# A planner that may take later TensorE products first, and single PSUM banks in turn

## The chip, the cores and the metric

The kernel runs on one core of a Trainium2 chip. The metric is the device time of one execution in microseconds (us). A change of about 0.2% can be told from none.

## What is computed

Three parts follow one another: retention (attention with a decaying mask instead of a softmax), a feed-forward layer with a softmax gate and a layer norm, and four experts whose outputs are weighted per token. Cut to what matters:

```python
scores = (q @ k.T) / sqrt(64)                 # 4 sequences of 576 tokens, 8 heads of 64
x = (scores * decay_mask) @ v                 # no softmax; -> 2304 tokens x 512
h = x @ w_in                                  # 512 -> 1024
e = exp(h - max(h)); solu = h * e / (sum(e) + 1e-9)
x2 = layernorm(solu) * g_ln @ w_out           # 1024 -> 512
p = domain_probs / (sum(domain_probs) + 1e-9)
for e in range(4):
    out += p[:, e:e+1] * (relu(x2 @ w1[e]) @ w2[e])   # 512 -> 1024 -> 512
```

## The kernel before

The 2304 tokens are 18 groups of 128 and go through in three passes of six groups (two blocks of 384 tokens). A product in near full precision is made of three matmuls with operands split in a high and a low part (mm3). A pass has these stages:

- h and t: for each group h_mm makes two halves of h in a PSUM tile of two banks (next_a, two such tiles, psA); chain1 to chain3b are the softmax gate and the norm on VectorE, ScalarE and GpSimd; t_mm transposes the result into two banks, t_hi and t_lo (or t_los) split it into hT.
- x2: x2_mm(b, m) makes a 128 x 384 piece of the second projection from hT and wB (24 matmuls, one bank); x2_act, x2_dve and x2_new turn the pieces into the sums B11 ... T4 that the experts multiply with (a Strassen-like scheme of seven products).
- experts: pass one (experts, with l1 and l2_mm) keeps tokens on the partitions in its second layer; passes two and three (experts_s) use the seven products for both layers and take transformed weights back from DRAM. A step of l1 has the products 1, 5, 2, 6, 4 (of the step before), 3, 7, each two times three matmuls of 384 columns. Its PSUM banks are x (for products 1, 6, 7, 4), y (5, 3) and z (2). l2_mm makes 24 matmuls of 512 columns into one bank, and l2_out adds the result to acc.

PSUM has eight banks: three single ones (bt, called b in the profile; next_b takes them in turn), sbank, and four that a pool holds, either as two double tiles (psA) or as four single ones (psX). Opening a pool closes the one before; its tiles wait for the last use of the tiles that lay there.

Retention of the first eleven groups lies in the head of the kernel, whose order is written out by hand (ORDER) and issued directly. The last seven groups (OWN) are taken in during the last expert of pass one and the h stage of pass two: att_pre loads the group and scales v and q on GpSimd, att_first makes the state and the scores (att_st, att_qk), att_last the output (att_pv). Their buffers are tmp and dec in turn.

From the end of the head on, nothing is issued directly: the class Recorder notes each operation with its engine, a modelled cost and the operations it depends on. flush then plays the recorded operations through a model of the engines and issues them in the order that comes out. Every PE operation has a due time, its place on a clock of PE work in program order; other operations are due early enough for what follows them, or 12 us (SLACK) after their place. Each engine takes of its ready operations the one due first, with one exception: TensorE keeps the order of the program,

```python
if e == "PE":
    can = [r for r in can if r[2] is pe[at]]
```

A flush is a border: nothing behind it is planned before anything ahead of it on the same engine. Such borders stand before the last expert's second layer in pass one, before xb is laid out in pass two (i == GP - 1), at the start of experts_s and at its end.

Nearly all instructions have line L144 in the profile, the recorder's call, so tiles tell them apart.

Of the kernel before, what the change touches and what calls it, by code (L numbers as in the profile page):

```python
# [26 lines left out]
GP = NG // NPASS  # L27
TB = GP // 2
# [31 lines left out]
l4 t5 r3 l5 s1 s3  # L60
"""

LATENCY = 0.12
ISSUE = 0.06
FIXED = {"PE": 0.0135, "ACT": 0.13, "DVE": 0.16, "POOL": 0.36, "SP": 2.0}
RATE = {"PE": 1 / 2400, "ACT": 0.93e-3, "DVE": 1.03e-3, "POOL": 1.82e-3, "SP": 4 * P / 300e3}
# [26 lines left out]
class Recorder:  # L93

    def __init__(self, nc):
        self.nc = nc
        self.ops = None
        self.seen, self.count = {}, 0
        self.now = 0.0
        self.free = {e: 0.0 for e in FIXED}  # L100
        self.port = self.dma = 0.0
        self.busy = {}
        for name, engine in ENGINE.items():
            setattr(self, name, Issuer(self, name, engine))

    def start(self):
        self.ops = []

    def note(self, op, ap, write):
        name, runs = spans(ap)  # L110
# [15 lines left out]
    def record(self, name, engine, kind, args, kw):  # L126
        aps = dict(kw)
        aps.update(zip(("out", "in0", "in1") if kind == "matmul" else ("out", "in_"), args))
        outs = [aps[k] for k in ("out", "accum_out") if isinstance(aps.get(k), bass.AP)]
        keys = ("in_", "in0", "in1", "scalar", "scalar1", "scalar2", "bias", "scale")  # L130
        ins = [aps[k] for k in keys if isinstance(aps.get(k), bass.AP)]
        size = lambda ap: int(np.prod([d[1] for d in tuple(ap.ap)[1:]]))
        n = size(aps["out"])
        if engine == "SP" and aps["out"].space == bass.MemoryType.DRAM:
            n = size(aps["in_"])
        elif kind == "tensor_reduce":
            n = size(aps["in_"])
        rate = RATE[engine]
        if engine == "PE" and aps["in0"].dtype == F32:
            rate *= 2 if kw.get("is_transpose") else 4  # L140
        call = getattr(getattr(self.nc, name), kind)
        wide = [a for a in ins if a.space != bass.MemoryType.PSUM and size(a) > 1]
        port = engine == "POOL" or (engine == "DVE" and len(wide) > 1)
        op = Op(engine, lambda: call(*args, **kw), FIXED[engine] + rate * n, port)  # L144
        op.banks = {a.name for a in ins + outs if a.space == bass.MemoryType.PSUM}
        for a in ins:
            self.note(op, a, False)
        for a in outs:
            self.note(op, a, True)
        op.before.discard(op)  # L150
        op.index = self.count
        self.count += 1
        self.ops.append(op)

    def flush(self, done=True):
# [2 lines left out]
        begin = clock  # L158
        inside = set(ops)
        for op in ops:  # L160
            op.after, op.due, op.at = [], None, clock
            if op.engine == "PE":
                op.due = clock
                clock += op.cost
# [24 lines left out]
        while len(order) < len(ops):  # L189
            late = now + 1e-9  # L190
            while waiting and waiting[0][0] <= late:
                op = heapq.heappop(waiting)[2]
                queue[op.engine].append((op.due, op.index, op))
            moved = False
            for e in FIXED:
                if free[e] > late or not queue[e] or (e == "SP" and self.dma > late + DEPTH):
                    continue
                can = [r for r in queue[e] if not (r[2].port and self.port > late)]
                can = [r for r in can if all(busy.get(b, 0) <= late for b in r[2].banks)]
                if e == "PE":  # L200
                    can = [r for r in can if r[2] is pe[at]]
                if not can:
                    continue
                best = min(can)
                queue[e].remove(best)
                op = best[2]
                moved = True
                if e == "PE":
                    at += 1
                    idle += now - max(free[e], begin)  # L210
                if e == "SP":
                    free[e] = now + ISSUE
                    self.dma = max(self.dma, now) + op.cost - FIXED[e]
                    op.end = self.dma + FIXED[e]
                else:
                    op.end = free[e] = now + op.cost
                if op.port:
                    self.port = op.end
                for b in op.banks:
                    busy[b] = op.end if e == "PE" else op.end + LATENCY  # L220
                op.start = now
                order.append(op)
                for s in op.after:
                    left[s] -= 1
                    ready_at[s] = max(ready_at[s], op.end + (0 if s.engine == e != "SP" else LATENCY))
                    if not left[s]:
                        heapq.heappush(waiting, (ready_at[s], s.index, s))
            if not moved:
                times = [*free.values(), self.port, self.dma - DEPTH, *busy.values(), *(w[0] for w in waiting[:1])]
                now = min(t for t in times if t > late)  # L230
# [17 lines left out]

SLACK = 12.0
DEPTH = 2.0  # L250
TRACE = []


@with_exitstack
def retention_solu_moe(
# [19 lines left out]
    big = ctx.enter_context(tc.tile_pool(name="big", bufs=1))  # L275
    drp = ctx.enter_context(tc.tile_pool(name="drp", bufs=1, space=bass.MemoryType.DRAM))
    psB = ctx.enter_context(tc.tile_pool(name="psB", bufs=1, space=bass.MemoryType.PSUM))
    stack = ExitStack()
    ctx.enter_context(stack)
    pool = {}  # L280

    def open_pool(name, bufs):
        stack.close()
        new = stack.enter_context(tc.tile_pool(name=name, bufs=1, space=bass.MemoryType.PSUM))
        width = 2048 // bufs
        pool["a"] = [new.tile([P, width], F32, tag=f"a{i}", name=f"{name}_{i}") for i in range(bufs)]
        pool["n"] = 0

    bt = [psB.tile([P, 512], F32, tag=f"b{i}", name=f"b{i}") for i in range(3)]
    sbank = psB.tile([P, 512], F32, tag="s", name="sbank")  # L290
    turn = [0]
    open_pool("psA0", 2)

    def next_a():
# [3 lines left out]
    def next_b():  # L298
        turn[0] += 1
        return bt[turn[0] % 3]  # L300

    def quad(t):
        return t.rearrange("p (n t) -> p n t", n=4)
# [224 lines left out]
            eng.tensor_tensor(out=t[:, 2560:3072], in0=t[:, 2560:3072], in1=t[:, 0:512], op=ALU.mult)  # L528

    def att_qk(g):  # L530
        t = grp(g)
        qt, kt = (t[:, i : i + 512].rearrange("p (n t) -> p n t", n=NP) for i in (0, 512))
        qk = [quad(next_b()) for a in range(2)]
# [13 lines left out]
        att[g] = ret  # L547

    def att_st(g):
        t = grp(g)  # L550
        kn, vd = (t[:, i : i + 512].rearrange("p (h t) -> p h t", h=H) for i in (1024, 2048))
        j = g % NJ
# [13 lines left out]
                copy(states[(g + 1) % 2][r, :, r], st_ps[r])  # L566

    def att_pv(g):
        t = grp(g)
        v = t[:, 1536:2048].rearrange("p (h t) -> p h t", h=H)  # L570
        qd = t[:, 2560:3072].rearrange("p (n t) -> p n t", n=NP)
# [68 lines left out]
    ln = {}  # L640

    def h_mm(g, n):
        if n == 0:
            hps[g] = next_a()
        ps = hps[g][:, 512 * n : 512 * n + 512]
# [53 lines left out]
    tps = {}  # L699

    def t_mm(g):
        y = exs[:, g % 3]
        if g % GP < (TB if g < GP else TB + 1):
            tps[g] = [quad(next_b()) for _ in range(2)]
        else:
            t = next_a()
            tps[g] = [quad(t[:, 512 * u : 512 * u + 512]) for u in range(2)]
# [45 lines left out]
    x2ps = {}  # L753

    def x2_mm(b, m):
        lt = hT[b]
        sl = slice(m * P, m * P + P)
        ps = next_b()[:, 0:BLK]
        for f in range(KF):
            w = wB[:, f]  # L760
            mm3(ps, (w[:, 0, sl], w[:, 1, sl]), (lt[:, 0, f], lt[:, 1, f]), f == 0, f == KF - 1)
# [120 lines left out]
    steps = {}  # L882

    def prod(s, i, bank, more=False):
        a, b = PRODUCTS[i]
        for kk in range(2):
            mm3(
# [17 lines left out]
    def l1(s, i):  # L905

        m = s % NM
        if i == 1:
            x = next_a()[:, 0:BLK]
            y, z = (next_b()[:, 0:BLK] for _ in range(2))  # L910
            steps[s] = (x, y, z)
        x, y, z = steps[s]
        if i == 1:
# [44 lines left out]
    FORDER = [0, 4, 1, 5, 2, 6, 3, 7]  # L958

    def l2_mm(ps, b, t, fs, first, last):  # L960
        sl = slice(t * P, t * P + P)
        for f in fs:
            h, w = hT[b], wB[:, f]
# [5 lines left out]
    def experts(p):  # L969
        for e in range(E):  # L970
# [9 lines left out]
                        l1(s - 1, 4)  # L980
                        w1_next(s + 2)
            last = s0 + NM - 1
            first = next_b()
            l2_mm(first, 1, 0, FORDER[:2], True, False)
            l1(last, 4)
            w1_next(last + 3)
# [10 lines left out]
            for b in (1, 0):  # L997
                for t in range(TB):
# [1 line left out]
                        ps, first = first, None  # L1000
                        l2_mm(ps, b, t, FORDER[2:], False, True)
                    else:
                        ps = next_b()
                        l2_mm(ps, b, t, FORDER, True, True)
                    l2_out(p, e, b * TB + t, ps)
                    if e + 1 == E:
# [59 lines left out]
    def experts_s(p):  # L1066
        wBf = wB.rearrange("p f s t -> p (f s t)")
        hTf = [t.rearrange("p s k t -> p (s k t)") for t in hT]
        nc.flush()
        open_pool(f"psX{p}", 4)  # L1070
        nc.start()
        xs = [t[:, 0:BLK] for t in pool["a"]]
        ys = [t[:, 0:BLK] for t in bt]
        zs = [sbank[:, 0:BLK]]
# [18 lines left out]
        at = {}  # L1093

        def mms(kind, k, i, ks):
            if (k, i) not in at:
                at[k, i] = used[kind]
                used[kind] += 1
# [147 lines left out]
                        x_load(p + 1, g)  # L1246
        nc.flush()
        if p + 1 < NPASS:
            open_pool(f"psA{p}", 2)
            nc.start()  # L1250

    OWN = list(range(EARLY, NG))
# [32 lines left out]
    def second(p, g0):  # L1285

        if p == 0:
            raw = tmp[:, 2048:3072]
            w1_load(0)
            w1_load(1, raw)  # L1290
            xb_region()
            nc.start()
            w1_ops(0)
            w1_ops(1, raw)
        else:
            for m in range(4):
                x2_mm(0, m)
                x2_act(m)
# [16 lines left out]
    with tc.manual_schedule():  # L1315
# [43 lines left out]
            atoms[atom[0]](int(atom[1:]))  # L1359
        second(0, None)  # L1360
        experts(0)
        for p in range(1, NPASS):
            g0 = p * GP
            own = p == 1
# [119 lines left out]
```

## Time and profile before

| | |
|---|---|
| median of 3 runs | 1041.54 us (1040.85 to 1042.57) |
| profiled execution | 1042.08 us |
| its span, first to last instruction | 1040.3 us |
| TensorE matmuls | 6188, busy 1008.3 us (97%) |
| VectorE, ScalarE, GpSimd busy | 617.3, 526.9, 445.6 us |
| mean granted TensorE clock | 0.996 of 2.4 GHz |

The profiled execution is one run; the differences below are taken against it. A matmul's end in the profile is modelled, and neighbours overlap, so the count of matmuls in a stretch tells more than the busy share. PEld is TensorE's weight load, which runs ahead of the matmuls. Idle time in brackets behind an instruction is that of its engine just before it, with the instruction that ended it.

### The profile page before, as it was taken

The page shows a single profiled execution, that of the slowest core. Times are in us where ns is not written, and L with a number is a line of the kernel's source. Part 1 is how long each engine was busy: PE and PEld are TensorE (multiplying, and loading weights), DVE is VectorE, ACT ScalarE, POOL GpSimd, SP SyncE. Part 2 cuts the span into 40 slices and gives each one's busy share as a digit, 9 for nine tenths or more (in the row PEclk, how much of TensorE's full clock was granted, in tenths as well). Part 3 has the DMA queues.
Part 4 walks back from the last instruction along what each step waited for, and adds up shares of the span by engine and source line. Part 5 has one row for each costly group of instructions (what it writes and reads, how often), then busy time and mean ns, then how long its engine had stood idle before and what let it go on. Part 6 is the DMA issues. An engine that isn't in the chain of part 4 may idle for free.

```text
span 1040.3 us, 17080 instructions
## 1 busy us (share of the span) xinstructions
PE 1008.3 (97%) x6188; PEld 947.0 (91%) x6188; DVE 617.3 (59%) x1038; ACT 526.9 (51%) x1032; POOL 445.6 (43%) x433
## 2 busy tenths in 40 slices
PE   4899999999999999999999999999999999999998
PEld 3788998898988987889999999999899999999998
DVE  6999686585774513643735656475444636556564
ACT  4568664262533402563745556473573746555462
POOL 2333354333635011321465655654230465655553
PEclk9999999999999999999999999999999999999999
DMA  9857689999785858551757666577640847566524
GB/s 343 343 186 257 216 293 313 309 292 336 227 270 185 280 226 304 203 200 59 232 152 226 184 195 211 157 270 248 243 152 18 250 134 244 163 216 193 184 72 134
DMA packets 122788, 226.79 MB, mean 218 GB/s; under 512 B 9936, under 2 KB 57040, under 8 KB 116560
## 3 DMA queue, kind: packets, MB, share of 16 engines
q1 hardware_dynamic: 122704, 225.70, 65.2%
q8 instruction: 49, 0.80, 0.3%
q14 instruction: 35, 0.29, 0.1%
HBM read 169.00 MB, written 62.95 MB: 223 GB/s over the span
## 4 chain that ended last, share of the span: by engine, by line
PE 51%; issue 1%; DVE 0%; ACT 0%; POOL 0%; POOLq 0%; ACTq 0%
PE psX L144 26%; PE b L144 16%; PE sbank L144 6%; PE psA L144 3%; DVE acc L144 0%; POOL acc L144 0%; DVE stats L144 0%; ACT psA L144 0%; ACT acc L144 0%; DVE tmp L144 0%; ACT xb L144 0%; ACT xa L144 0%; ACT tmp L144 0%; POOLq L144 0%; ACTq L144 0%
## 5 line engine op out<-in xcount | busy, mean ns | idle before, releaser
L144 POOL TENSOR_TENSOR h<-tmp,h 128x384 fp32r<-128x384 f32 x128 | 128.7, 1015 | 95.9 <-ACT h L144 82.1
L144 PE MATMUL b<-xa,wA 128*128 128x384 f32 x672 | 132.8, 335 | 2.3 <-DVE h L144 1.2
L144 PE MATMUL b<-wB,h 128*128 128x512 f32 x576 | 133.0, 390 | 1.3 <-POOL wB L144 1.3
L144 PEld LDWEIGHTS b<-wB,h 128*128 128x128 f32 x576 | 107.8, 188 | 24.2 <-POOL wB L144 2.2
L144 POOL TENSOR_TENSOR wA<-wA 128x512 fp32r<-128x512 f32 x74 | 97.2, 1321 | 68.0 <-ACT wA L144 65.0
L144 PEld LDWEIGHTS b<-xa,wA 128*128 128x128 f32 x672 | 117.7, 188 | 3.5 <-DVE h L144 2.1
L144 PE MATMUL psX<-xb,wA 128*128 128x384 f32 x576 | 112.6, 336 | 0.1
L144 PEld LDWEIGHTS psX<-xb,wA 128*128 128x128 f32 x576 | 100.4, 188 | 2.7 <-DVE b L144 2.3
L144 POOL TENSOR_TENSOR tmp<-tmp 128x256 f32<-128x256 f32 (+1 forms) x68 | 61.9, 925 | 72.0 <-DMA tmp<-in_w 50.0
L144 ACT ACTIVATE h<-tmp 128x384 fp32r<-128x384 f32 x144 | 72.9, 521 | 33.7 <-DVE tmp L144 33.7
L144 PE MATMUL b<-h,wB 128*128 128x384 f32 x480 | 85.1, 336 | 0.0
L144 PEld LDWEIGHTS b<-h,wB 128*128 128x128 f32 x480 | 83.0, 188 | 0.1
L144 PE MATMUL psX<-h,wA 128*128 128x384 f32 x408 | 74.9, 334 | 0.0
L144 DVE TENSOR_TENSOR sbank<-sbank,tmp 128x384 f32<-128x384 f32 x48 | 27.2, 566 | 77.4 <-PE sbank L144 54.3
L144 ACT ACTIVATE wA<-wA 128x512 fp32r<-128x512 f32 x74 | 46.3, 632 | 51.5 <-DMA wA<-sw 41.7
L144 ACT ACTIVATE tmp<-b 128x384 f32<-128x384 f32 x104 | 51.1, 491 | 41.8 <-DVE b L144 17.1
L144 PEld LDWEIGHTS psX<-h,wA 128*128 128x128 f32 x408 | 71.1, 188 | 0.0
L144 PE MATMUL psA<-wA,xa 128*128 128x512 f32 x288 | 70.2, 399 | 0.8 <-DVE tmp L144 0.7
L144 DVE TENSOR_TENSOR b<-b,tmp 128x384 f32<-128x384 f32 x80 | 45.0, 563 | 41.1 <-PE b L144 38.0
L144 PEld LDWEIGHTS psA<-wA,xa 128*128 128x128 f32 x288 | 53.6, 190 | 13.3 <-DVE tmp L144 1.0
L144 POOL TENSOR_TENSOR wC<-wC 128x512 fp32r<-128x512 f32 x38 | 50.6, 1337 | 31.8 <-ACT wC L144 31.8
L144 DVE SCALAR_TENSOR_TENSOR tmp<-b,tmp 128x384 f32<-128x384 f32 x96 | 51.2, 554 | 16.9 <-ACT tmp L144 8.5
(239 smaller groups left out, 1984.4 us busy)
## 6 DMA issues: line engine op xcount, KB each, us to landing
wA<-sw SPq DMA_DIRECT2D x298, 256.0 KB, 3.0
sw<-wA SPq DMA_DIRECT2D x32, 896.0 KB, 7.7
tmp<-in_w SPq DMA_DIRECT2D x24, 512.0 KB, 5.7
grps<-in_qkv SPq DMA_DIRECT2D x10, 1024.0 KB, 6.5
wC<-sw SPq DMA_DIRECT2D x38, 256.0 KB, 2.8
sw<-wCf SPq DMA_DIRECT2D x32, 256.0 KB, 3.3
wA<-sin SPq DMA_DIRECT2D x8, 1024.0 KB, 6.7
wB<-sout SPq DMA_DIRECT2D x8, 1024.0 KB, 8.0
```

The source lines that it names most:

```text
L144: op = Op(engine, lambda: call(*args, **kw), FIXED[engine] + rate * n, port)
```

## The change

- Costs: LATENCY 0.15 instead of 0.12; a float32 matmul that is no transpose costs 2 instead of 4 units per column; a VectorE operation with two operands in SBUF costs 1.2 times as much.
- Order on TensorE: mark() numbers the products (each att_, h_, t_, x2_, prod and l2 call is a group). The planner may now take any ready PE operation up to 150 recorded operations (AHEAD) behind the first one not issued, and stays in a group it has begun while it has something ready there.
- Pass one's experts: the pool of four banks is opened as four single tiles (psX0) ahead of x2's second block, and x, y, z and the second layer's banks come from next_x, which goes round the seven banks psX and bt. x2's second block uses it too.
- After pass one's experts: a flush, and psA1 is opened as two double tiles.
- Passes two and three: the flush and the opening of the single tiles move from the start of experts_s to the start of second, ahead of x2. There x2's first block and the last two transposed groups use next_s (bt and sbank in turn), its second block next_x.

The diff, cut to its core:

```diff
-LATENCY = 0.12
+LATENCY = 0.15
...
         if engine == "PE" and aps["in0"].dtype == F32:
-            rate *= 2 if kw.get("is_transpose") else 4
+            rate *= 2
...
+        rate *= 1.2 if engine == "DVE" and port else 1.0
...
                 if e == "PE":
-                    can = [r for r in can if r[2] is pe[at]]
+                    while at < len(pe) and pe[at].start is not None:
+                        at += 1
+                    can = [r for r in can if r[2].index <= pe[at].index + AHEAD]
+                    can = [r for r in can if r[2].group == self.last] or can
...
+AHEAD = 150
...
+    def next_s():
+        turn[2] += 1
+        return (bt + [sbank])[turn[2] % 4]
+
+    def next_x():
+        turn[1] += 1
+        return (pool["a"] + bt)[turn[1] % 7]
...
     def t_mm(g):
+        nc.mark()
         y = exs[:, g % 3]
-        if g % GP < (TB if g < GP else TB + 1):
+        if g >= GP and g % GP >= GP - 2:
+            tps[g] = [quad(next_s()) for _ in range(2)]
+        elif g % GP < (TB if g < GP else TB + 1):
             tps[g] = [quad(next_b()) for _ in range(2)]
...
     def x2_mm(b, m):
+        nc.mark()
...
-        ps = next_b()[:, 0:BLK]
+        ps = (next_b if nc.ops is None else next_x if b else next_s)()[:, 0:BLK]
...
         if i == 1:
-            x = next_a()[:, 0:BLK]
-            y, z = (next_b()[:, 0:BLK] for _ in range(2))
+            x, y, z = (next_x()[:, 0:BLK] for _ in range(3))
...
-            first = next_b()
+            first = next_x()
...
-                        ps = next_b()
+                        ps = next_x()
...
     def experts_s(p):
-        nc.flush()
-        open_pool(f"psX{p}", 4)
-        nc.start()
...
         if p + 1 < NPASS:
-            open_pool(f"psA{p}", 2)
+            open_pool("psA2", 2)
...
             xb_region()
+            open_pool("psX0", 4)
             nc.start()
             w1_ops(0)
             w1_ops(1, raw)
         else:
+            nc.flush()
+            open_pool(f"psX{p}", 4)
+            nc.start()
             for m in range(4):
                 x2_mm(0, m)
...
         experts(0)
+        nc.flush()
+        open_pool("psA1", 2)
+        nc.start()
```

## Rows read from the trace of the kernel before

**Rows 1.** Page, part 1: busy us of each engine, share of the span, instructions.

```profile
PE 1008.3 (97%) x6188; PEld 947.0 (91%) x6188; DVE 617.3 (59%) x1038; ACT 526.9 (51%) x1032; POOL 445.6 (43%) x433
```

**Rows 2.** Busy us (instructions) by stretch and engine, clock, DMA share, GB/s.

```profile
125.00:385.00 260.00, 255.84 (x1288) 230.51 (x1288) 161.82 (x266) 103.97 (x200) 102.55 (x97) 1.00 0.85 279
385.00:455.00 70.00, 66.67 (x618) 55.31 (x618) 32.95 (x55) 27.93 (x49) 15.09 (x23) 0.98 0.54 203
497.00:728.00 231.00, 230.85 (x1326) 229.37 (x1324) 131.39 (x240) 127.45 (x264) 130.52 (x114) 1.00 0.66 210
...
800.00:1036.00 236.00, 234.90 (x1349) 233.32 (x1348) 134.17 (x244) 130.26 (x270) 130.83 (x115) 1.00 0.57 176
```

**Rows 3.** Waits of TensorE, 120 to 1040 us: us in total, times, longest.

```profile
PE sbank L144 <- POOL tmp L144: 2.4, 1, 2.4
PE b L144 <- POOL wB L144: 1.3, 2, 0.7
PE b L144 <- DVE h L144: 1.2, 2, 0.7
PE psA L144 <- DVE h L144: 1.1, 1, 1.1
PE b L144 <- ACT xb L144: 1.1, 1, 1.1
PE b L144 <- DVE tmp L144: 0.9, 2, 0.7
PE psA L144 <- DVE tmp L144: 0.7, 1, 0.7
PE psA L144 <- ACT tmp L144: 0.5, 1, 0.5
```

**Rows 4.** Chain that ended last: start us, us, what; two undisturbed pieces.

```profile
498.00 1.04 PE b L144 x6
...
753.07 5.47 PE psA L144 x24
```

**Rows 5.** Timeline 340 to 343 us: start, us, engine, operation [idle before].

```profile
340.19 1.21 PE L144 MATMUL psA<-xb,wA 128*128 128x384 f32 x6
...
342.50 1.34 PE L144 MATMUL psA<-xa,wA 128*128 128x384 f32 x6 [1.10 <-DVE h L144]
```

**Rows 6.** Timeline 214 to 217 us: two starts where the weight load idled shortly.

```profile
214.45 1.01 PEld L144 LDWEIGHTS psA<-xa,wA 128*128 128x128 f32 x6 [0.30 <-DVE h L144]
214.45 1.32 PE L144 MATMUL psA<-xa,wA 128*128 128x384 f32 x6
...
216.71 1.00 PEld L144 LDWEIGHTS b<-xa,wA 128*128 128x128 f32 x6 [0.22 <-DVE h L144]
```

**Rows 7.** Timeline 389 to 407 us, and the stretch 400 to 420 us.

```profile
389.69 1.01 SPq L144 DMA_DIRECT2D wB<-sout  x2
...
394.32 0.37 SPq L144 DMA_DIRECT2D tmp<-in_qkv  x1
...
395.36 1.16 PE L144 MATMUL b<-dec 64*128 64x128 f32 x16
...
402.70 1.04 POOL L144 TENSOR_TENSOR tmp<-tmp,tabs 128x512 f32<-128x512 f32 x1 [23.83 <-DMA tmp<-in_qkv]
...
404.41 1.96 PE L144 MATMUL b<-tmp 64*128 64x128 f32 x16
...
406.30 4.01 PE L144 MATMUL psA<-wA,xa 128*128 128x512 f32 x13
...
400.00:420.00 20.00, 17.58 (x164) 14.74 (x161) 8.33 (x13) 6.17 (x11) 6.57 (x9) 0.91 0.79 305
```

**Rows 8.** Timeline at 496.7 us, start of pass two's experts.

```profile
496.66 1.01 PEld L144 LDWEIGHTS psX<-xb,wA 128*128 128x128 f32 x6 [0.41 <-ACT tmp L144]
```

**Rows 9.** Timeline 458 to 464 us: x2's start in pass two.

```profile
458.01 6.27 PE L144 MATMUL b<-h,wB 128*128 128x384 f32 x34
...
461.51 1.28 DVE L144 TENSOR_TENSOR h<-b,h 128x512 fp32r<-128x512 f32 x2
```

More of the change, by code (lines that the diff above doesn't have):

```diff
@@ L98, in __init__ @@
         self.seen, self.count = {}, 0
+        self.group, self.last = 0, None
         self.now = 0.0
@@ L107, in start, with mark @@
         self.ops = []
+    def mark(self):
+        self.group += 1
     def note(self, op, ap, write):
@@ L150, in record @@
         op.before.discard(op)
+        op.group = self.group
         op.index = self.count
@@ L160, in flush @@
         for op in ops:
-            op.after, op.due, op.at = [], None, clock
+            op.after, op.due, op.at, op.start = [], None, clock, None
             if op.engine == "PE":
@@ L208, in flush @@
                 if e == "PE":
-                    at += 1
+                    self.last = op.group
                     idle += now - max(free[e], begin)
@@ L277, in retention_solu_moe @@
     psB = ctx.enter_context(tc.tile_pool(name="psB", bufs=1, space=bass.MemoryType.PSUM))
+    turn = [0, 0, -1]
     stack = ExitStack()
@@ L287, in open_pool @@
         pool["n"] = 0
+        turn[1] = -1
     bt = [psB.tile([P, 512], F32, tag=f"b{i}", name=f"b{i}") for i in range(3)]
     sbank = psB.tile([P, 512], F32, tag="s", name="sbank")
-    turn = [0]
     open_pool("psA0", 2)
@@ L568, in att_pv @@
     def att_pv(g):
+        nc.mark()
         t = grp(g)
@@ L642, in h_mm @@
     def h_mm(g, n):
+        nc.mark()
         if n == 0:
@@ L701, in t_mm @@
     def t_mm(g):
+        nc.mark()
         y = exs[:, g % 3]
-        if g % GP < (TB if g < GP else TB + 1):
+        if g >= GP and g % GP >= GP - 2:
+            tps[g] = [quad(next_s()) for _ in range(2)]
+        elif g % GP < (TB if g < GP else TB + 1):
             tps[g] = [quad(next_b()) for _ in range(2)]
@@ L755, in x2_mm @@
     def x2_mm(b, m):
+        nc.mark()
         lt = hT[b]
         sl = slice(m * P, m * P + P)
-        ps = next_b()[:, 0:BLK]
+        ps = (next_b if nc.ops is None else next_x if b else next_s)()[:, 0:BLK]
         for f in range(KF):
@@ L884, in prod @@
     def prod(s, i, bank, more=False):
+        nc.mark()
         a, b = PRODUCTS[i]
@@ L960, in l2_mm @@
     def l2_mm(ps, b, t, fs, first, last):
+        nc.mark()
         sl = slice(t * P, t * P + P)
@@ L1095, in mms @@
         def mms(kind, k, i, ks):
+            nc.mark()
             if (k, i) not in at:
```

## The prediction

> **What bounds the kernel now.** I read the busy table first: TensorE is busy for 97% of the span [rows 1], so no other engine's work is worth anything unless TensorE waits for it. Then the table by stage, to see where its idle time lies behind the hand-ordered head (0 to 125 us): pass one's experts keep it busy for 255.84 of 260 us, the attention of the tokens that follow for 66.67 of 70, while the experts of passes two and three have 230.85 of 231 and 234.90 of 236 [rows 2]. The diff leaves the head's order alone (it is issued directly, without the planner), so the head's idle time is no part of the sum. Then TensorE's own waits from 125 us on: those shown add up to 2.4 + 1.3 + 1.2 + 1.1 + 1.1 + 0.9 + 0.7 + 0.5 = 9.2 us, in eleven waits [rows 3]. That is all the change can work on, apart from what a wait costs beyond its idle time.
>
> That extra has to be priced, because a busy TensorE is modelled. A product of six 384-column matmuls advances the chain by 1.04 us (0.173 each) when nothing is in the way [rows 4]. Round a wait, the product before it is booked with 1.21 us, 0.17 of it tail that would have overlapped, and the product after it with 1.34, so 0.13 more [rows 5]. The waiting matmul also holds back the weight load behind it. So a wait costs its idle time plus about 0.17 + 0.11 = 0.28 us (0.11 is what the second start loses, 1.34 - 1.21 rounded down). I use 0.28 for each.
>
> **The change part by part.**
>
> *Single banks in pass one.* Before, a step's products sat in one of two double-width tiles (x) and two of three single banks (y, z); the next step's y or z is a bank just left. Rows 5 show what that does: the matmul into psA at 342.50 waits 1.10 us until VectorE has read the step before out of that tile. Waits of this kind are "b, DVE h" (1.2 us, two) and "psA, DVE h" (1.1 us, one) [rows 3]: 2.3 + 3 x 0.28 = 3.1 us. Two shorter ones show only in the weight load's idle time, 0.30 and 0.22 us [rows 6]; less the tail of 0.17 and plus the 0.11 of the second start (1.32 against 1.21 again) that is 0.24 and 0.16: 0.4 us. With seven banks in turn, the bank for a new product was last used more than two steps (over 14 us) ago, so all 3.6 us should go. Bounds: 2.6 (one wait kept) to 3.6; I take 3.6. The second layer of pass one gets the same seven banks; its evictions already keep up, so nothing.
>
> *Later work first, in pass one.* The waits for data are "b, POOL wB" (1.3 us, two: the split second-layer weights come late) and "psA, ACT tmp" (0.5, one): 1.8 + 3 x 0.28 = 2.6 us [rows 3]. Free banks let TensorE take the next tile's ready products meanwhile. But the instruction order is fixed when the program is written, so a wait is filled only if the planner's costs foresee it. The change makes VectorE's two-operand work dearer and the latency 0.15, which helps; GpSimd's cost is untouched. Bounds 0 to 2.6; I take half, 1.3.
>
> *The stall at 403.8.* This is the dearest one: TensorE idles 2.4 us for GpSimd, which idles until 402.70 for a transfer into tmp that SyncE issued at 394.32, behind two 1 MB loads issued at 389.69 [rows 3, 7]. The granted clock of 400 to 420 us is 0.91 [rows 7]: a stretch at the 1.2 GHz level follows the idle time. Its cost: the qk group takes 1.96 us against 1.16, and thirteen matmuls 4.01 us where 24 take 5.47 with their tail left out (0.228 each, so 2.96 + 0.17 = 3.13): 0.80 + 0.88 = 1.7 us [rows 4, 7]. Together 2.4 + 0.28 + 1.7 = 4.4 us. Two parts act on it. The planner may now put half an h product (12 x 0.228 = 2.7 us) ahead of the waiting state product. And a new flush after pass one puts the four 1 MB loads behind the tmp load in SyncE's order, so that the latter has the DMA engines to itself; what moves behind it is needed only at x2, 50 us later. Bounds 1.7 (only the clock's part) to 4.4; I take 4.0.
>
> *Attention's next wait*, "b, DVE tmp" (0.9 us in two, so 1.2 with one refill of 0.28) [rows 3]: h products are ready, if the planner sees the wait. 0 to 1.2; I take 0.7.
>
> *x2 and the experts in one plan.* Before, a flush stood between them. The waits there are "b, ACT xb" (1.1 + 0.28) [rows 3] in pass three and one in pass two that shows as 0.41 us of idle time of the weight load [rows 8], 0.41 - 0.17 + 0.11 = 0.35 us by the same working. B11 and B21 are ready long before, so other products can go first: 0 to 1.7; I take 1.2.
>
> *What it adds.* First, the new pool after pass one must wait for the last evictions, as pass three's does now ("psA, DVE tmp", 0.7 + 0.28) [rows 3]. Here two attention groups stand between the last expert tile and the first h product, so nothing; without that cover 0 to 1.0. Second, the fresh rotation of x2's banks: counting the turns, the first x2 product of pass two takes b0, where the second half of a transposed group was just written. In the trace that x2 product starts at 458.01, while VectorE reads that half until 461.51 + 1.28 = 462.8 [rows 9]. In program order this would hold TensorE, and everything queued behind it on TensorE, for 4.8 us + 0.28 = 5.1. The planner knows the bank and can take the next x2 product first (24 x 0.173 = 4.2 us): 0.6 to 0.9 is left. Bounds 0 to 5.1; I take 0.6. Third, products moved forward start just when the plan calls them ready, with no slack. The trace doesn't show such starts; the nearest row is the shortest breaks [rows 6, 8], 0.2 to 0.3 us each. Bounds 0 to 20 of them (5.6 us); I take 7, 2.0 us. The moved flushes themselves issue no instruction; ScalarE, VectorE and GpSimd have idle time to take them [rows 2].
>
> Sum: -3.6 - 1.3 - 4.0 - 0.7 - 1.2 = -10.8, and +0.6 + 2.0 = +2.6, net **-8.2 us**. The profiled execution took 1042.08 us (span 1040.3, 1.8 around it), the median run 1041.54. From the profiled one 1033.9, from the median 1033.3; I say 1033.4. The best end is all gains and no cost, -3.6 - 2.6 - 4.4 - 1.2 - 1.7 = -13.5, so 1028.0.
>
> **The rivals.** *Slower: slack lost in the dense stages.* From 497 to 728 and 800 to 1036 us TensorE runs 2675 matmuls in 467 us, 0.1746 each against the undisturbed 0.173 [rows 2, 4]; that is about 340 products with next to nothing to win. If the planner, with its new costs, thinks one late that is not, it moves another forward that is ready only on paper, and TensorE waits on the chip with all later products queued behind it. A wait of 0.3 us costs 0.3 + 0.28 = 0.58; 14 of them (one in 24) eat the 8.2 us, 25 make it 1042.1 - 8.2 + 14.5 = 1048.4. For it: the plan's costs are averages, and VectorE's order is rebuilt too. Against it: where the head of the order is ready and due first it keeps its place, and a program order that runs here without a wait is mostly ready in the plan as well. *It doesn't do what it says.* The planner sees none of the waits, so the order stays and only banks and flushes act: -3.6 - 1.7 + 1.0 + 3.5 (most of the blocked x2 product) = -0.8, so 1041.2. For it: waits of half a microsecond are below what such costs foresee. Against it: the 2.4 us stall is far above that.
>
> *The clock.* Half a microsecond to a microsecond of idle time in pass one left the granted clock at 1.00 [rows 2, 3]; only the stage with the 2.4 us stall fell. The Trainium skill (TensorE: Matmul & The Clock Gate, A second HAM failure mode) tells of a kernel that cycled through PSUM banks and fell back in clock through small idle gaps, which speaks against this change; the dense stages rotate through all eight banks at a clock of 1.00 [rows 2], so the trace doesn't agree. Were more small gaps to bring one stretch at 1.2 GHz into each of the four experts of pass one, each at the 1.7 us above: 1033.4 + 6.8 = 1040.2.
>
> **How the numbers follow.** Forecast 0.68 (alone 1028.0 to 1038.5), no effect 0.12, lost slack 0.16, clock 0.04. The range runs from the best end, 1028.0, to 1042.0: it takes in the forecast, the no-effect case and the clock, and leaves out most of the slack case and a little below. A measurement of this kernel tells 0.2%, 2.1 us, from no change: faster is under 1039.5, slower over 1043.6. Faster: the forecast less a little, and some of the others, 0.70. Same: most of the no-effect and clock cases and the mild part of lost slack, 0.14. Slower: 0.16.
>
> **What would show it.** Right: no wait for "DVE h" in pass one; clock 1.00 from 400 to 420 us; TensorE busy near 259 of 260 us in pass one's experts; the x2 products of pass two's start swapped. Wrong: new waits of b, psX or sbank in the dense stages (lost slack); the same waits as before outside the banks' (no effect); a stall near 458 us of some 5 us; a granted clock below 1.00 in new places.

## The result and the profile after

| | before | changed |
|---|---|---|
| median (runs) | 1041.68 us (6) | 1030.74 us (6) |
| lowest to highest | 1035.68 to 1042.57 | 1028.85 to 1033.13 |
| ratio, 95% interval | | 0.9904 [0.9877, 0.9932] |
| second comparison | 1039.7 us (7) | 1029.41 us (4), 0.9897 [0.9882, 0.9912] |
| profiled execution, its span | 1042.08, 1040.3 | 1028.85, 1027.1 |

The change saves 10.9 us (10.3 in the second comparison); 8.2 were forecast, and 1030.7 lies in the range of 1028.0 to 1042.0. Ratios here and below are of means, so they differ a little from the quotients of the medians. The instructions on TensorE are the same 6188 matmuls. First the busy table and TensorE's waits behind 120 us (in us: total, times, longest) of the changed kernel, to be held against [rows 1, 3]:

```profile
PE 1006.8 (98%) x6188; PEld 949.4 (92%) x6188; DVE 616.2 (60%) x1038; ACT 526.4 (51%) x1032; POOL 448.4 (44%) x433
```

```profile
PE psA L149 <- DVE tmp L149: 0.6, 1, 0.6
PE b L149 <- DVE h L149: 0.5, 1, 0.5
PE psA L149 <- ACT psA L149: 0.2, 1, 0.2
```

Of the eleven waits with 9.2 us, and a twelfth of 0.2 us (psA for ScalarE's psA) that [rows 3] leave out, three with 1.3 us are left. Two of the three stood there before (0.7 and 0.2); the one of 0.5 us for VectorE's h, in pass three, is new. None is in pass one's experts or in attention. The table by stretch (busy us and instructions of PE, PEld, DVE, ACT, POOL; granted clock; DMA share; GB/s) shows the same:

```profile
125.00:375.00 250.00, 250.00 (x1273) 228.46 (x1273) 161.48 (x264) 101.35 (x198) 98.98 (x96) 1.00 0.86 288
375.00:444.00 69.00, 68.89 (x623) 56.02 (x622) 31.69 (x53) 27.52 (x48) 15.41 (x24) 1.00 0.55 203
486.50:716.00 229.50, 229.50 (x1326) 229.46 (x1324) 132.36 (x242) 128.69 (x267) 131.62 (x115) 1.00 0.67 211
790.00:1024.00 234.00, 232.96 (x1344) 232.64 (x1343) 134.96 (x246) 130.26 (x270) 131.36 (x115) 1.00 0.58 178
```

And the first of these stretches of the kernel before:

```profile
125.00:375.00 250.00, 245.84 (x1244) 222.23 (x1244) 160.49 (x265) 103.97 (x200) 99.01 (x94) 1.00 0.87 285
```

Read the counts, not the busy time: in 250 us of pass one TensorE gets 1273 matmuls done instead of 1244. The dense stage of pass two takes 229.5 us for the 1326 matmuls that took 231 [rows 2].

Since ends of matmuls are modelled, I also work out lost time. It is a matmul's start less the undisturbed pitch of all matmuls ahead of it (0.1733 us for 384 columns, 0.2267 for 512, 0.1092 for a transposed block, 0.0555 and 0.0295 for attention's two small shapes). Taken at the same amount of work, it shows by stage where two executions part, whatever the order. It is worked out from the traces and is no view of the profile:

```
lost us within       before  before   changed changed  program order,
                     (1st)   (again)  (1st)   (again)  free bank (e11)
head                 30.6    32.5     29.2    28.8     31.2
pass one's experts    7.6     7.5      0.6     1.5      5.4
attention, h          9.9     8.4      7.9     7.9      6.8
x2 of pass two        0.6     0.5      0.5     0.5      0.2
dense, pass two       1.1     1.1      0.0     0.0      1.5
h, x2 of pass three   3.2     3.2      2.6     2.6      1.9
dense, pass three     5.3     5.4      4.3     4.3      5.6
whole span           58.3    58.7     45.1    45.7     52.7
```

Pass one's experts are taken from the second block of its x2 on, where the planner begins. Attention ends with the last transposed group ahead of the first x2 product, x2 with the first products of the experts behind it; the last dense stage holds the 4.3 us behind the last matmul too. The head is the same code in all of them and differs by up to 4 us; over all executions of this study it loses 28.5 to 33.3. That is why single spans (here 13.2 us apart) say less than the medians, and why a comparison of stages behind the head is sharper than one of times.

### The profile page after: what moved, and what is told of

Same layout as the page of the kernel before. It is cut to its first block, busy times and chain, and to the rows that moved or that the text cites. A ratio compares the mean times of both kernels' runs of the same rounds, so it can differ in the third digit from the quotient of the medians.

```text
span 1027.1 us, 17077 instructions
## 1 busy us (share of the span) xinstructions
PE 1006.8 (98%) x6188; PEld 949.4 (92%) x6188; DVE 616.2 (60%) x1038; ACT 526.4 (51%) x1032; POOL 448.4 (44%) x433
## 4 chain that ended last, share of the span: by engine, by line
PE 93%; DVE 4%; DMA 2%; ACT 1%; SPq 0%; issue 0%; ACTq 0%
PE psX L149 44%; PE b L149 29%; PE sbank L149 8%; PE psA L149 6%; DMA dec<-in_w_in 1%; DMA sx<-wA 1%; PE b L382 1%; PE b L384 1%; PE b L383 1%; PE b L604 1%; DVE wA L387 1%; PE psA L383 1%; PE psA L382 1%; PE b L610 1%; PE psA L384 0%; PE b L557 0%
## 5 line engine op out<-in xcount | busy, mean ns | idle before, releaser
L149 PE MATMUL psX<-xb,wA 128*128 128x384 f32 x738 | 143.7, 334 | 0.0
L149 PEld LDWEIGHTS psX<-xb,wA 128*128 128x128 f32 x738 | 129.4, 188 | 0.3
L149 PE MATMUL b<-xa,wA 128*128 128x384 f32 x564 | 111.0, 334 | 0.0
L149 PEld LDWEIGHTS b<-xa,wA 128*128 128x128 f32 x564 | 99.0, 188 | 0.1
L149 ACT ACTIVATE tmp<-psX 128x384 f32<-128x384 f32 x122 | 59.5, 489 | 53.0 <-PE psX L149 51.1
L149 POOL TENSOR_TENSOR tmp<-tmp 128x256 f32<-128x256 f32 (+1 forms) x68 | 56.9, 853 | 57.1 <-DMA tmp<-in_w 38.3
L149 PE MATMUL psX<-wB,h 128*128 128x512 f32 x336 | 78.9, 390 | 0.0
L149 PE MATMUL psX<-xa,wA 128*128 128x384 f32 x396 | 77.4, 334 | 0.0
L149 ACT ACTIVATE tmp<-b 128x384 f32<-128x384 f32 x108 | 53.1, 492 | 42.5 <-DVE b L149 18.4
L149 PEld LDWEIGHTS psX<-wB,h 128*128 128x128 f32 x336 | 63.0, 188 | 12.8
L149 PEld LDWEIGHTS psX<-xa,wA 128*128 128x128 f32 x396 | 69.5, 188 | 0.2
```

## The experiments

All ratios are to the kernel before, run on the same chip beside the kernel in question.

**Second profiles.** Both kernels unchanged.

> The kernel before, unchanged, for a second profile of it. Theory one (the 2.4 us stall with its slow stretch is a fixed part of the kernel): a wait for GpSimd's tmp of 2 us or more and a granted clock under 0.95 between 400 and 420 us, as in the first profile. Rival (the stall's size and the slow stretch differ from execution to execution, which is why the added flush didn't show in the time): a wait under 1.5 us, or a clock of 1.00 there; all other waits behind 125 us within 0.2 us of the first profile.

> The changed kernel, unchanged, beside the next two on the same chip. Theory one: 9 to 12 us less than the kernel before, TensorE busy for all of pass one, the three waits behind 125 us of its first profile again (0.6, 0.5 and 0.2 us). Rival (the first result was half luck of the head): under 7 us.

The changed kernel came out at 0.9897 [0.9882, 0.9912]; its waits are those of the first profile with one more, in pass one:

```profile
PE psX L149 <- DVE h L149: 0.6, 1, 0.6
```

The product starts at 335.68, when VectorE has read a tile of the pool into h (an operation of 0.55 us from 335.07 on). So even with seven banks in turn a wait of the kind that the banks should cure can stand there; e5 and e6 below have one too, of 0.7 and 0.6 us. The kernel before showed another picture at the stall:

```profile
PE sbank L144 <- POOL tmp L144: 1.4, 1, 1.4
...
PE sbank L144 <- POOL dec L144: 0.8, 1, 0.8
```

```profile
400.00:420.00 20.00, 17.75 (x175) 14.61 (x174) 8.16 (x13) 6.17 (x11) 7.12 (x9) 1.00 0.87 330
```

The wait is 1.4 us instead of 2.4, another of 0.8 has joined it, and the granted clock is 1.00 where the first profile had 0.91 [rows 7]. The other waits agree within 0.2 us. So the stretch at 1.2 GHz, 1.7 us of my sum, belonged to one execution and not to the kernel.

**Program order (e1).**

```diff
-AHEAD = 150
+AHEAD = 0
```

> The changed kernel with AHEAD at 0, so that TensorE keeps the program's order again; banks, costs and flushes stay as changed. Theory one (banks and order each carry a part): pass one's bank waits stay gone (3.6 us), but its waits for data return (up to 2.6), attention's waits return in part (about 2), the first x2 product of pass two is held by its bank for about 5 us, and the step from x2 to the experts waits again (about 1.5): some 11 us above the changed kernel, 1040 to 1043 us, no gain over the kernel before. Rival (banks and costs did it, the order adds little): 1031 to 1033 us.

1042.64 us, 1.0021 [1.0007, 1.0035]: slower than the kernel before, so theory one holds for the time. Not for all its parts: pass one loses 5.1 us and x2 of pass two 6.2, but attention loses 6.7, less than the changed kernel's 7.9, and no wait of 1.5 us stands between x2 and the experts. The timeline of TensorE at x2's start in pass two (start us, us, engine, operation, idle time before) shows the dearest part:

```profile
453.18 1.03 PE L149 MATMUL b<-tabs,acc 128*128 128x128 f32 x8
458.81 9.91 PE L149 MATMUL b<-h,wB 128*128 128x384 f32 x48 [4.59 <-DVE h L149]
```

The first x2 product waits until VectorE has read the transposed group out of its bank. The granted clock of 444 to 486 us is 0.96 in this run, so part of it ran at 1.2 GHz, as behind the stall in the first profile.

**Program order, free bank (e11).** As e1, and x2's rotation starts one bank further on in pass two:

```diff
             nc.flush()
             open_pool(f"psX{p}", 4)
+            turn[2] = 1 - p
             nc.start()
...
-AHEAD = 150
+AHEAD = 0
```

> TensorE in the program's order (AHEAD at 0) with x2's bank rotation of passes two and three starting at a bank that is free; else as changed. Theory one (what the program's order lost against the kernel before at x2's start was the blocked bank alone, 4.6 us of idle time and 0.3 of restart): that wait goes, 4.9 us less than the run in program order, so a ratio to the kernel before of 0.9965 to 0.9985, which is what banks, costs and flushes are worth without the free order. Rival (the wait moves to the next x2 product, which queues behind the same evictions): a new wait for VectorE's h of over 2 us within 10 us of x2's start, and a ratio above 1.0.

1034.27 us, 0.9951 [0.9930, 0.9973]. The wait went and no other came in its place, so theory one holds in kind. In size the step from e1 to e11 is 0.0070, 7.3 us, more than the 4.9 expected: the trace puts 6.0 us of it at x2's start (6.2 us lost there in e1, 0.2 here), of which 4.6 + 0.3 are the wait. The rest fits the clock, which is 1.00 again; in e1 the 48 matmuls behind the wait take 9.91 us, 1.4 more than undisturbed (48 x 0.1733 and 0.17 of tail).

```profile
444.00:486.00 42.00, 42.00 (x267) 40.37 (x266) 18.11 (x32) 22.06 (x41) 10.60 (x13) 1.00 0.43 155
```

Banks, costs and flushes alone are therefore worth some 5 us once the rotation does no harm, and the free order another 5 (0.9951 against 0.9904 and 0.9897). By the table that is 4.4 us in pass one and 2.8 in the dense stages; attention goes the other way and loses 1.1 more with the free order, and x2 loses 1.0 more in the two passes, where e11 also has the free bank. In pass one the free order cures what banks can't. These waits for data are left there in e11,

```profile
PE b L149 <- POOL wB L149: 1.4, 2, 1.0
...
PE b L149 <- DVE xb L149: 0.9, 1, 0.9
...
PE psX L149 <- POOL wB L149: 0.7, 1, 0.7
```

while no wait for VectorE's h is left there. From the first product of the experts on, pass one loses 3.7 us in e11 against 6.9 and 6.8 before: 3.1 us for the banks, together with the new costs, which no run takes apart here. Ahead of that product e11 loses 1.0 more than before (the wait for xb is new), so over the whole stage 2.1 us are left.

**Old banks in pass one (e2).** Free order, costs and flushes as changed:

```diff
-        ps = (next_b if nc.ops is None else next_x if b else next_s)()[:, 0:BLK]
+        ps = (next_b if len(pool["a"]) == 2 else next_x if b else next_s)()[:, 0:BLK]
...
-            x, y, z = (next_x()[:, 0:BLK] for _ in range(3))
+            x = next_a()[:, 0:BLK]
+            y, z = (next_b()[:, 0:BLK] for _ in range(2))
...
-            first = next_x()
+            first = next_b()
...
-                        ps = next_x()
+                        ps = next_b()
...
-            open_pool("psX0", 4)
```

> The changed kernel, but pass one keeps its banks of before: two double tiles for x, three single banks for y, z and the second layer. Order, costs and flushes as changed. Theory one: the bank waits of pass one return, at most their 3.6 us, less what TensorE can fill with other work: 1032.5 to 1034.5 us, and waits for VectorE's h in the profile between 125 and 375 us. Rival (with a free order the banks no longer matter): 1030.5 to 1031.5 us and TensorE busy for all of pass one.

1029.50 us, 0.9909 [0.9880, 0.9938]: the time of the changed kernel, so the rival is right on the time. In the trace one wait is left in pass one,

```profile
PE b L149 <- ACT wB L149: 1.1, 1, 1.1
```

and the stretch from 125 to 375 us has 1265 matmuls, between the 1244 of before and the 1273 of the changed kernel. No wait for VectorE's h is among them. With a free order TensorE finds other work while a bank is read; the seven banks are then worth 1 to 2 us at most (2.4 us lost in pass one against 0.6 to 1.5). In the time even that is hidden, since attention loses 6.6 us in e2 and not 7.9.

**Old costs (e3).**

```diff
-LATENCY = 0.15
+LATENCY = 0.12
...
-            rate *= 2
+            rate *= 2 if kw.get("is_transpose") else 4
...
-        rate *= 1.2 if engine == "DVE" and port else 1.0
```

> The changed kernel with the planner's old costs (latency 0.12, float32 matmuls at 4 units, VectorE's two-operand work without the 1.2). Theory one (foresight by the costs fills the waits for data): one to three of those waits return, 1 to 2.5 us: 1031.5 to 1033 us. Rival A (costs don't matter): 1030 to 1031.5 us. Rival B (the costs are the main part, since without them the free order puts work where it isn't ready): over 1036 us.

1033.02 us, 0.9936 [0.9915, 0.9957], 3.3 us above the changed kernel's first ratio, with intervals that overlap (that of the second comparison lies just below). The trace has three kinds of waits that the changed kernel doesn't have, so theory one, at the upper end of its range:

```profile
PE b L148 <- ACT tmp L148: 1.4, 1, 1.4
PE sbank L148 <- POOL tmp L148: 0.9, 1, 0.9
...
PE b L148 <- DVE tmp L148: 0.6, 3, 0.3
```

These with 0.28 each are 4.3 us of waits, of which the stages behind the head show about 1.3 as more lost time than the changed kernel's; how much of the 3.3 is the costs stays open between 1.3 and 3.3.

**Less reach (e7).**

```diff
-AHEAD = 150
+AHEAD = 40
```

> The changed kernel with AHEAD at 40 recorded operations instead of 150. At the start of the second pass's x2 the next product that could stand in for the blocked one lies about 64 operations behind it. Theory one (what is gained in pass one needs only the next product or two, and x2's swap needs the long reach): pass one stays within 1 us of the changed kernel's, the wait for VectorE's h at x2's start in pass two is back at 3.5 to 5 us, 1033 to 1036 us if the kernel before takes 1040. Rival (40 reaches everything): within 1.5 us of the changed kernel, 1029 to 1031.5.

1039.92 us, 1.0000 [0.9988, 1.0012]: the whole gain is gone, more than theory one expected. Pass one keeps most of its part (248.18 of 250 us busy, 1268 matmuls), but loses 2.6 us, 1.1 to 2.0 more than the changed kernel where at most 1 was expected; attention loses 1.2 more. The wait at x2's start is back with the expected length, but x2 loses 8.2 us against 0.5, because of the clock and a second wait of 0.5 us:

```profile
457.80 15.24 PE L149 MATMUL b<-h,wB 128*128 128x384 f32 x72 [4.60 <-DVE h L149]
```

```profile
444.00:486.50 42.50, 37.36 (x215) 35.43 (x214) 12.84 (x22) 18.24 (x33) 9.56 (x12) 0.92 0.41 146
```

A mean of 0.92 with two levels means that 16% of these 42.5 us, 6.8 us, ran at 1.2 GHz. Part of that falls into the wait itself: the 72 matmuls behind it take 15.24 us where 72 x 0.1733 and 0.17 of tail make 12.65, so 2.6 us were lost on top of the wait. TensorE gets 215 matmuls done there, the changed kernel 250.

**The flush alone (e4).** The kernel before with one line more:

```diff
         experts(0)
+        nc.flush()
+        nc.start()
         for p in range(1, NPASS):
```

> The kernel before with one flush added after pass one's experts; nothing else. Theory one (SyncE's order cures the 2.4 us stall at 403.8 and the slow stretch behind it, since the four 1 MB loads now come behind the load into tmp): 3 to 4.4 us less than before, 1037.3 to 1038.7 us, and a clock of 1.00 in that stretch. Rival (only TensorE's free order cures it): 1041 to 1042 us, the wait for GpSimd's tmp still over 1.5 us.

1040.30 us, 1.0007 [0.9994, 1.0021]. In its trace the wait for GpSimd's tmp is 0.8 us and the clock did not fall, as theory one has it, but the time doesn't move. The second profile of before explains most of this: against its 1.4 and 0.8 us there is little to cure. Lost time shows that little: attention loses 7.3 us in e4, against 9.9 and 8.4 before, and 1.2 us is less than these times can tell. The step "SyncE's order cures a stall of 4.4 us" was built on an unlucky execution.

**Attention as one group (e5).**

```diff
     def att_qk(g):
-        nc.mark()
         t = grp(g)
...
     def att_st(g):
-        nc.mark()
         t = grp(g)
```

> The changed kernel with the state, score and output products of neighbouring attention groups in one group for the planner, so that TensorE goes from the 512-column products to attention's small shapes 7 times instead of 13 in the second pass's h stage. Theory one (each such excursion costs about 0.3 us in starts, which is where most of the attention part of the gain went): 1.5 to 2 us less than the changed kernel. Rival (the products are put together where the transfers and GpSimd haven't come yet): new waits for GpSimd's tmp or dec of over 0.5 us, and a time equal or longer.

1031.82 us, 0.9921 [0.9897, 0.9945], not shorter. Theory one falls, and not by the rival's waits either: none for tmp or dec is there. The excursions did become fewer, 8 instead of 12, but the 432 small matmuls take 28.4 us in them instead of 26.0. Timelines of one excursion of 64 in the kernel before (again), and in this one:

```profile
394.77 1.09 PE L144 MATMUL b<-tmp 128*64 128x128 f32 x16
395.69 1.04 PE L144 MATMUL b<-tmp,st 128*64 128x128 f32 x16
396.57 0.63 PE L144 MATMUL sbank<-dec 128*64 128x64 f32 x16
397.13 1.16 PE L144 MATMUL b<-dec 64*128 64x128 f32 x16
398.22 3.04 PE L144 MATMUL psA<-wA,xa 128*128 128x512 f32 x12
```

```profile
395.64 1.15 PE L149 MATMUL b<-dec 128*64 128x128 f32 x16
396.57 1.09 PE L149 MATMUL b<-dec,st 128*64 128x128 f32 x16
397.59 1.16 PE L149 MATMUL b<-tmp 64*128 64x128 f32 x14
398.68 0.73 PE L149 MATMUL sbank<-tmp 128*64 128x64 f32 x16
399.34 0.49 PE L149 MATMUL b<-tmp 64*128 64x128 f32 x2
399.75 0.50 PE L149 MATMUL psA<-wA,xa 128*128 128x512 f32 x1
```

398.22 - 394.77 = 3.45 us against 399.75 - 395.64 = 4.11 us for the same 64 matmuls: within a group the planner takes the operation due first, so the state product cuts the score product in two, which adds two changes between shapes. That these cost the time fits the rows; no run tests it alone.

**Program order inside a group (e9).**

```diff
-                best = min(can)
+                if e == "PE" and can[0][2].group == self.last:
+                    best = min(can, key=lambda r: r[1])
+                else:
+                    best = min(can)
```

> The changed kernel, but inside a group that TensorE has begun it takes the operation that stands first in the program, not the one that is due first. Theory one (attention's 432 small matmuls run slower where the order mixes the two kinds of an output product: 1.95 us for 32 of them against 1.74 in the program's order): the output products fall back to about 1.75 us, 7 x 0.2 = 1.2 to 1.4 us less in attention, 1028 to 1029.5 us if the kernel before takes 1040. Rival (the small matmuls' time is set by what stands round them): output products still at 1.9 us or more, and no difference over 0.5 us.

1028.88 us, 0.9892 [0.9874, 0.9911]; by the time it can't be told from the changed kernel. An excursion of 32 goes from 1.95 to 1.89 us and from 1.75 to 1.71; all small matmuls from 26.0 to 25.45 us. So the direction is theory one's, the size about half of it, and its reason doesn't hold: in all but the first excursion the two kinds of an output product already stand apart in the changed kernel, sixteen and sixteen, and in the first they are mixed in both. What changed is the order inside each kind. On the size, I had compared 1.95 us of an excursion of its own with 1.74 us inside a longer one.

**Free banks (e6), and both (e10).** e6 is the changed kernel with

```diff
-        if g >= GP and g % GP >= GP - 2:
+        if g >= GP and g % GP == GP - 1:
+            tps[g] = [quad(next_x()) for _ in range(2)]
+        elif g >= GP and g % GP == GP - 2:
             tps[g] = [quad(next_s()) for _ in range(2)]
...
+            pool["n"] = 1
             nc.start()
...
+            turn[2] = 1 - p
             nc.start()
```

e10 has these edits and that of e9.

> The changed kernel with three bank choices altered: pass three's first h product takes the tile over banks 0 and 1 of the pool, which were left long before; the last transposed group of a pass takes two psX banks; x2's rotation starts at a bank that is free. Theory one (the 0.6, 0.5 and one 0.3 us waits left are bank waits): these waits go with their 0.28 us each, 1.5 to 2.3 us less than the changed kernel. Rival (the data behind them, VectorE's last gathers and the low halves, come just as late): within 0.7 us.

> The program's order inside a group and the free banks for x2 and the last transposed groups together (of the run with three bank choices, the first h product of pass three didn't start earlier; the wait for VectorE's h in pass three and the swap in pass two went). Theory one: the gains add, 1.2 to 1.4 of attention and 0.8 of the transposed groups, some 2 us less than the changed kernel, 1027.5 to 1029 us if the kernel before takes 1040. Rival: the head's differences between executions hide both, within 0.7 us of the changed kernel.

e6: 1029.45 us, 0.9893 [0.9874, 0.9912]. e10: 1029.20 us, 0.9890 [0.9871, 0.9909]. The wait of 0.5 us for VectorE's h in pass three went, that of 0.6 to 0.7 us at pass three's first h product did not, though its tile lay over banks left long before:

```profile
719.95 0.56 DVE L149 TENSOR_TENSOR tmp<-psX,pb 128x384 f32<-128x384 f32 x1 [0.26 <-PE psX L149]
...
720.57 3.68 PE L149 MATMUL psA<-wA,xa 128*128 128x512 f32 x15 [0.65 <-DVE tmp L149]
```

It starts when VectorE has read a tile of the old pool, as if the new pool as a whole waited for the old one; no run tests that further. Neither run can be told from the changed kernel by its time, and the trace of e9 has the shortest span of all, 1025.7 us. Behind the head, though, the changed kernel loses 15.9 and 16.9 us in its two traces, e9 15.2, e6 15.8 and e10 14.2: the gains do add there, and the head hides them in the time.

## Why the prediction was right

**Pass one: right in sum, wrong in what did it.** The bank waits (3.6 taken, 2.6 to 3.6; the two terms shown, 3.1 and 0.4, make 3.5) and the waits for data (1.3 taken of 0 to 2.6) made 4.9; the traces show 6.0 to 7.1 less lost time. I had said that the banks do the first part and the planner's foresight half of the second. e11 comes near the price of the banks in program order, 3.1 us from the first product of the experts on, with the new costs. But e2 shows that the free order takes 5.1 of the 6.5 us without them. The two parts of the change overlap; the waits for data all went, and of the sign "no wait for DVE h in pass one" the first profile of the changed kernel has none, the second one of 0.6 us.

**The stall at 403.8: the term that was mis-sized.** I took 4.0 of 4.4 us, and 0.7 for the next wait. The waits of attention did go, all of them. But attention and its h stage went from 9.9 and 8.4 us lost to 7.9, so 2.0 against the profile I had and 0.5 against the second one. Two things failed. The price held a slow stretch of one execution (1.7 us). And the free order filled the waits as I had said, with half an h product of twelve matmuls, but this splits attention's small matmuls: they come in 12 excursions instead of 8, as here,

```profile
406.33 0.73 PE L149 MATMUL sbank<-dec 128*64 128x64 f32 x16
406.99 1.16 PE L149 MATMUL b<-dec 64*128 64x128 f32 x16
408.08 3.06 PE L149 MATMUL psA<-wA,xa 128*128 128x512 f32 x12
411.07 1.15 PE L149 MATMUL b<-dec 128*64 128x128 f32 x16
```

and each excursion has late starts at both its ends: 0.09 us at its first matmul, 0.15 at the first 512-column matmul behind it and 0.11 at the second. An excursion of 64 with its return loses 0.57 us in the kernel before (394.77 to 401.19); the same kinds, 64 in two excursions, lose 1.06 (406.33 to 415.97). The first one, of 96 matmuls from 382.6 on, loses 2.4 us alone. So this stage owes its gain to something else: in program order it loses 6.8 us (e11), and the kernel before with the flush alone 7.3 (e4).

**x2: right.** The first x2 product of pass two meets its bank, the planner swaps in the next one, and no wait is left:

```profile
446.76 1.03 PE L149 MATMUL b<-tabs,acc 128*128 128x128 f32 x8
447.55 4.43 PE L149 MATMUL b<-h,wB 128*128 128x384 f32 x24
```

With the start of the experts x2 loses as much as before in pass two (0.5 us) and, with the h stage, 0.6 less in pass three; 1.2 less 0.6 were forecast. The two waits that I had counted (0.35 and 1.4 us with their extra) are gone. What came in their place is not the swap, which costs nothing, but 0.4 us at a late start in pass two (466.6) and the new wait of 0.5 us in pass three, which e6's banks take away. The bound for the other case, 5.1 us, was too low: x2 loses 6.0 us more in e1 than in e11 and 7.7 more in e7 than in the changed kernel, with 1.2 GHz behind the wait. That TensorE idles 4.6 us while a product in a free bank stands right behind the blocked one agrees with the Trainium skill (TensorE: Matmul & The Clock Gate, Step-by-step: what each phase is for), by which only weight loads are pulled ahead and matmuls stay in program order.

**Starts without slack: the cost that didn't come.** I added 2.0 us. The dense stages lose 1.0 us less in each of the two passes, since a break of 0.24 us (two late starts, by the trace) once per expert, eight in all, which I had counted as next to nothing, is gone too. The slower rival fell with it: no wait stands in the dense stages.

**The clock.** Rotating through seven banks left the granted clock at 1.00 in pass one. So the trace doesn't bear out the rival that I had named with the Trainium skill (TensorE: Matmul & The Clock Gate, A second HAM failure mode: psum-queue depth-cycling). Between the head and the last matmul the clock fell only at single waits of 2.4 us (in the one profile that has it) and 4.6 us; a wait of 1.8 us in pass one of e7 left it at 1.00.

So the forecast was -4.9 (pass one), -4.7 (attention), -0.6 (x2) and +2.0 (starts), in all -8.2 us. The lost time behind the head moved by -6.5, -1.3, -0.7 and -2.1, means of two profiles each, in all -10.6: one term far too high, two too low, and x2 as forecast. That the sum came out within 2.4 us is in part luck, since the errors of attention (3.4) and of the starts (4.1) are opposite.

What stays open: how much of e3's loss is the costs, and how much the head's spread adds to any single comparison below 0.2%. The free order alone, with the old costs, banks and flushes, was not run.

## What to carry to other kernels

Where an engine that runs in order is 97% busy and its order is planned ahead, let the planner take later ready work: here it filled bank waits, data waits and stage borders at once, and left 1 to 2 us in one stage for the extra banks, which the time doesn't show. Give it reach enough to get past the worst collision (40 operations were too few, and one blocked product cost the whole gain), and look at what the free choice does to the shapes of neighbouring instructions: in attention it lost 1.1 us against the program's order. Take a second profile of the old kernel before pricing a single stall.

## What was not expected of the hardware

- A wait of 4.6 us on TensorE costs more than itself: 6.0 us with a granted clock of 0.96 over the 42 us round it (e1), 7.7 us with 0.92 (e7, with a second wait of 0.5). The wait and its place are the same in both; the stretch at 1.2 GHz is not: the matmuls behind the wait lose 1.4 us to it in e1 and 2.6 in e7.
- The same 64 small matmuls of attention take 3.45 us in one order and 4.11 us in another, with no wait in either.
- With the same code in the head, one execution loses 28.5 us there (e9) and another 33.3 (e10).
